# Attention heads and expert products on one TensorE: how far products may run ahead, and which engine splits the last weights

## The chip, the cores and the metric

The kernel runs on one core of one Trainium2 chip. The metric is the device time of one execution in microseconds; lower is better.

## The reference, cut to what matters

```python
# q, k, v: (4, 8, 576, 64) fp32, f: (4, 8, 576); w1: (4, 512, 1024), w2: (4, 1024, 512)
scores = q @ k.T / 8 + cum[:, None] - cum[None, :]      # cum = cumsum(log f), causal
attn = softmax(scores) ; a = attn @ v                     # 32 (batch, head) pairs
x = a with heads side by side: (2304, 512)
p = domain_probs / domain_probs.sum(-1)
out = sum over e of p[:, e] * (relu(x @ w1[e]) @ w2[e])   # 4 dense experts, 2304 tokens
```

## The kernel before

All matrix products are fp32 quality: each operand is split into a high part (a rounded copy, made on ScalarE) and a low part (the difference, made on VectorE or GpSimd), and three products high*high, high*low, low*high are summed in PSUM. TensorE therefore sees three matmuls for one, and the other engines make the parts.

Attention is cut into 64 heads, each a (batch, head) pair for one half of the queries: 32 early heads (half 0: the first 256 queries and keys) and 32 late heads (half 1: 320 queries against 576 keys). Two heads share one job, with one load of q and k (`load`, L235, into `raw`, one buffer) and one of v (L237). For a head, ScalarE copies the high part (L278), GpSimd casts q and makes the lower parts (L279, L287, L293), TensorE makes scores (L331), VectorE takes the minimum with the mask (L345), ScalarE the exponentials (L360), TensorE transposes (L423), ScalarE and VectorE split the result (L433, L440), TensorE multiplies with v (`av`, L473), and at the end of a job `fin` scales and stores the two heads.

Tokens lie in nine chunks of 256. Chunks 0 to 2 are multiplied directly while attention still runs: 48 steps (class `Step`), each a weight pair of one expert for one chunk, in eight quarter-steps (four `l1` at L639, four `l2` at L669), with a gate between on ScalarE and VectorE (L650, L651). Weights come in blocks of 1024 columns (`w_load`, L596, three buffers `wr`) and are split by `w_split`: the high part on ScalarE (L607), two lower halves of 128x512 on GpSimd or, for the blocks in W_DVE, on VectorE (L611). Six buffers hold split blocks (`wh`, `wl`); there are NS = 56 blocks. Chunks 3 to 5 and 6 to 8 form two sets. For a set `x_block` makes seven operands (four of them sums, L751 on GpSimd; high part L752, low part L753), and 16 weight pairs (class `Big`) follow, each with seven products of L815 and the second layer at L876. `big_split` makes a pair's weights: four sums on GpSimd (L769), high parts on ScalarE (L789), seven lower parts on GpSimd (L792), from the same three `wr` buffers and into the same six split buffers.

Order. The first eight heads (batch 0, half 0) run in `startup`, which is written out by hand slot by slot and keeps its order; its slots W_SLOT call `w_split` for blocks 0 to 3. After it the program order is made by `pace`: every piece of a head has a cost (an early head's `av` 1100, a late one's 600), and after each quarter-step as many pieces are emitted as the line through `marks` allows; all heads and the operands of set 0 are to be out AHEAD steps before the last. A scheduler then puts each engine's instructions in order by program order and by when it estimates them ready; each engine works its list in that order. `behind` ties each product to the heads: a quarter-step may be issued only after the last head instruction on TensorE that had been emitted LAG quarter-steps earlier. All DMAs are issued by SyncE in order.

Of the kernel before, what the change touches and what calls it, by code (L numbers as in the profile page):

```python
# [26 lines left out]
)  # L27
DIRECT = (0, 1, 2)
LEAD = 3
LAG = 5  # L30
W_DVE = tuple(range(4, 16, 2))
SETS = ((3, 4, 5), (6, 7, 8))
AHEAD = 4
W_SLOT = (5, 6, 7, 8)
NEAR = 2
JOBS = ((0, 0), (1, 0), (2, 0), (3, 0), (0, 1), (1, 1), (2, 1), (3, 1))

# [33 lines left out]
def fused(ctx: ExitStack, tc: tile.TileContext, qk, v, f, probs, w, out):  # L71
    nc = tc.nc
# [475 lines left out]
    heads = [(j, hh) for j in jobs for hh in range(2)]  # L548
    FIRST = 2 * NPR

    def head_steps(n):

        st = []
        if n + 1 < len(heads):
            j, hh = heads[n + 1]
            if hh == 0:
                st.append((0, j.prep_v))
            st.append((0, lambda j=j, hh=hh: j.prep(hh)))
        if n + 2 < len(heads):
            j, hh = heads[n + 2]  # L560
            st.append((0, lambda j=j, hh=hh: j.far(hh)))
        ahead = n + 2 < len(heads) and heads[n + 2][1] == 0
        if ahead:
            st.append((0, heads[n + 2][0].load))
        qs, ts, us = [], [], []
        if n < len(heads):
            j, hh = heads[n]
            for t in j.its:
                qs.append((TOK0[t] + 328, lambda j=j, hh=hh, t=t: j.qk_tile(hh, t)))
            if hh == 1:  # L570
                qs.append((0, j.recip))
        if n > FIRST:
            j, hh = heads[n - 1]
            for gi in range(len(j.blocks())):
                ts.append((500, lambda j=j, hh=hh, gi=gi: j.tr(hh, gi)))
            us.append(((1100, 600)[j.half], lambda j=j, hh=hh: j.av(hh)))
            if hh == 1:
                us.append((0, j.fin))
        if n + 1 < len(heads):
            j, hh = heads[n + 1]  # L580
            us.append((0, lambda j=j, hh=hh: j.begin(hh)))
        for k in range(max(len(qs), len(ts))):
            st += ts[k : k + 1] + qs[k : k + 1]
        return st + us
# [4 lines left out]
    NS = 4 * len(UNITS)  # L589
# [3 lines left out]
    def w_load(n):  # L593
        if n < NW and n not in wraw:
            wraw[n] = wr_p.tile([128, 1024], F32, tag="wr", name=f"wr{n}")
            nc.sync.dma_start(out=wraw[n], in_=w[ROWS[n]])  # L596

    def w_split(n):
        if n >= NS:
            if n % 2 == 0:  # L600
                big_split((n - NS) // 2)
            return
        w_load(n)
        wh[n] = w_p.tile([128, 1024], F32R, tag="wh", name=f"wh{n}")
        wl[n] = w_p.tile([128, 1024], F32R, tag="wl", name=f"wl{n}")
        r = wraw.pop(n)
        nc.scalar.activation(out=wh[n], in_=r, func=AF.Copy)  # L607
        for a in (0, 512):
            z = a + 512
            eng = nc.vector if n in W_DVE else nc.gpsimd  # L610
            i = eng.tensor_tensor(  # L611
                out=wl[n][:, a:z], in0=r[:, a:z], in1=wh[n][:, a:z].bitcast(F32), op=ALU.subtract
            )
            if eng is nc.gpsimd:
                latest["POOL"] = i
        w_load(n + 1)
        w_load(n + 2)
        w_load(n + 3)
# [118 lines left out]
    def x_block(n, k, a=None, z=None, op=None):  # L737

        hw = len(SETS[n]) * CH // 2
        hi = rh[n, k] = late.x.tile([128, 2, hw], F32R, tag=f"rh{k}", name=f"rh{n}_{len(rh)}")  # L740
        lo = rl[n, k] = late.x.tile([128, 2, hw], F32R, tag=f"rl{k}", name=f"rl{n}_{len(rl)}")
        x_of = lambda b: (
            xset[n][:, 2 * b[0] : 2 * b[0] + 2, hw * b[1] : hw * b[1] + hw]
            if type(b) is tuple
            else xs_[n, b]
        )
        if op is None:
            x = x_of(k)
        else:
            x = xs_[n, k] = late.x.tile([128, 2, hw], F32, tag="t", name=f"rx{n}_{k}", bufs=2)  # L750
            nc.gpsimd.tensor_tensor(out=x, in0=x_of(a), in1=x_of(z), op=op)  # L751
        nc.scalar.activation(out=hi, in_=x, func=AF.Copy)  # L752
        nc.vector.tensor_tensor(out=lo, in0=x, in1=hi.bitcast(F32), op=ALU.subtract)  # L753

# [3 lines left out]
    def big_split(p):  # L758
        if p >= 16 * len(SETS):
            return  # L760
        n = NS + 2 * p
        w_load(n)
        w_load(n + 1)
        r = [wraw.pop(n), wraw.pop(n + 1)]
        part = lambda b: r[b[0]][:, 256 * b[1] : 256 * b[1] + 256]
        t = late.x.tile([128, 4, 256], F32, tag="wt", name=f"wt{p}", bufs=1)
        w_of = lambda b: part(b) if type(b) is tuple else t[:, b - 1, :]
        for k, a, z, op in SUMS:
            nc.gpsimd.tensor_tensor(out=t[:, k - 1, :], in0=w_of(a), in1=w_of(z), op=op)  # L769
        tiles = []  # L770
        for k in range(3):
            tiles.append(
                [
                    w_p.tile([128, 1024], F32R, tag=x, name=f"b{x}{p}_{k}") for x in ("wh", "wl")
                ]
            )
        f = t.rearrange("p k n -> p (k n)")
        jobs_ = [
            (0, 0, f),
            (1, 0, part((1, 1))),  # L780
            (1, 256, part((0, 0))),
            (1, 512, part((0, 1))),
            (2, 0, r[0][:, 512:]),
            (2, 512, r[1][:, 512:]),
        ]
        for k, c, x in jobs_:
            w_ = x.shape[1]
            hi, lo = (y[:, c : c + w_] for y in tiles[k])
            nc.scalar.activation(out=hi, in_=x, func=AF.Copy)  # L789
            for a in range(0, w_, 512):  # L790
                z = min(a + 512, w_)
                nc.gpsimd.tensor_tensor(  # L792
                    out=lo[:, a:z], in0=x[:, a:z], in1=hi[:, a:z].bitcast(F32), op=ALU.subtract
                )
        bw[p] = tiles
        for k in range(2, 5):
            w_load(n + k)
# [103 lines left out]
    for x in X_ORDER:  # L901
        asteps.append((600, lambda x=x: x_block(0, *x)))
# [21 lines left out]
    goals = sorted((max(n - LEAD, 1), cost[need[c]]) for c, n in first.items() if n > 0)  # L924
    goals.append((len(steps) - AHEAD, cost[-1]))
    while goals:
# [17 lines left out]
    def startup():  # L944

        J = lambda h: heads[h] if 0 <= h < FIRST else (None, None)
        decays()
        for h in range(2):
            j, hh = J(h)
            if h == 0:  # L950
                j.prep_v()
            j.prep(hh)
        for h in range(2):
            J(h)[0].begin(h)
        heads[0][0].qk_pe(0, (0, 1))
        heads[0][0].qk_min(0, 0)
        heads[0][0].qk_min(0, 1)
        for s in range(FIRST + 2):
            (j, hh), (m, mm), (n, nn), (i, ii) = J(s), J(s + 1), J(s + 2), J(s - 2)
            if n:  # L960
                n.begin(nn)
                n.prep_hi(nn)
                n.prep_lo(nn)
            if m:
                m.qk_pe(mm, m.its)
                for t in m.its:
                    m.qk_min(mm, t)
            if j:
                for t in j.its:
                    j.qk_exp(hh, t)  # L970
            if i:
                i.av_pe(ii)
                i.av_top(ii)
                i.av_add(ii)
            if j:
                j.tr_pe(hh, 0)
                j.tr_hi(hh, 0)
                j.tr_lo(hh, 0)
                if hh == 1:
                    j.recip()  # L980
                if hh == 0 and s > 0:
                    j.prep_v()
            if s >= 5 and s % 2 == 1:
                heads[s - 4][0].fin()
            if s == FIRST + 1:
                heads[FIRST - 1][0].fin()
            if s in W_SLOT:
                w_split(W_SLOT.index(s))

    pt0 = [pt_p.tile([128, 1216], F32R, tag=x, name=f"{x}_first") for x in ("pth", "ptl")]  # L990
    with tc.manual_schedule():
        startup()

    with ExitStack() as after:
        for e in ("ACT", "DVE", "POOL"):
            i = latest[e]
            after.enter_context(tc.issue_after(i.ins))
        normalize()
        j = heads[FIRST][0]
        j.prep_v()  # L1000
        j.prep(0)
        j.begin(0)
        for n in range(len(W_SLOT), 6):
            w_split(n)
# [5 lines left out]
    def behind(act, q):  # L1010
        marks_pe.append(latest["PE"])
        with tc.issue_after(marks_pe[-min(len(marks_pe), LAG)].ins):
            act(q)
# [85 lines left out]
```

## Time and profile before

| | us |
|---|---|
| median of three runs (1040.11 to 1044.52) | 1042.0 |
| the profiled execution | 1039.19 |
| its span, first to last instruction | 1036.9 |
| TensorE busy | 982.1 (95%) |
| TensorE weight load busy | 882.5 (85%) |
| VectorE busy | 724.6 (70%) |
| GpSimd busy | 650.6 (63%) |
| ScalarE busy | 529.7 (51%) |
| mean granted TensorE clock | 0.988 |

The span is what the trace covers; the profiled execution is 2.3 us longer than its span, and the median of the runs is 2.8 us above the profiled execution. Busy time of TensorE counts a matmul until its modelled end, so a stretch that is fully busy may still hold small gaps: work is better counted in matmuls times their spacing.

### The profile page before, as it was taken

What the parts mean: (1) busy time and instruction counts of PE and PEld (TensorE: products, weight loads), DVE (VectorE), ACT (ScalarE), POOL (GpSimd) and SP (SyncE); (2) the same over time, 40 slices, a digit from 0 to 9 for tenths busy, and PEclk for the clock granted to TensorE, in tenths of its full rate; (3) what the DMA queues carried; (4) which work ended last, traced back from release to release, by engine and by line L of the source; (5) the groups of instructions that cost most, each with busy time, mean ns of one, the idle gap of its engine ahead of it and who ended that gap; (6) DMA issues with size and microseconds to landing.
All of it is one profiled execution on the core that took longest, in us unless ns stands there. A gap on an engine that the chain in (4) does not pass through costs nothing.

```text
span 1036.9 us, 15930 instructions
## 1 busy us (share of the span) xinstructions
PE 982.1 (95%) x5584; PEld 882.5 (85%) x5584; DVE 724.6 (70%) x1474; ACT 529.7 (51%) x1127; POOL 650.6 (63%) x690
## 2 busy tenths in 40 slices
PE   5788999999999999999699999999999999999998
PEld 4676878899998989999589887898988988988987
DVE  5668766676767777766447758766797777677665
ACT  6666767676766667675224333433343333433330
POOL 5756778563635475563977767676686766666640
PEclk9988999999999999999989999999999999999999
DMA  5344554342432343331321222112123222122101
GB/s 199 104 156 129 165 156 143 106 143 85 144 104 91 103 157 99 103 118 42 122 81 58 66 82 82 63 61 82 51 72 113 71 82 79 44 82 71 52 21 61
DMA packets 33903, 99.53 MB, mean 96 GB/s; under 512 B 3652, under 2 KB 5760, under 8 KB 33824
## 3 DMA queue, kind: packets, MB, share of 16 engines
q1 hardware_dynamic: 33824, 98.53, 29.2%
q8 instruction: 44, 0.72, 0.3%
q14 instruction: 35, 0.29, 0.1%
HBM read 93.64 MB, written 4.87 MB: 95 GB/s over the span
## 4 chain that ended last, share of the span: by engine, by line
PE 71%; POOL 7%; DVE 7%; issue 5%; ACT 5%; DMA 4%; SPq 0%; POOLq 0%; ACTq 0%; DVEq 0%
PE y L876 23%; PE m L815 20%; PE l L669 8%; PE l L639 7%; PE s L331 4%; PE t L423 4%; PE o L473 4%; DMA raw<-in_qk 2%; POOL wl L611 2%; POOL bwl L792 2%; DMA wr<-in_w 1%; ACT wh L607 1%; POOL wt L769 1%; ACT p L360 1%; DVE v L266 1%
## 5 line engine op out<-in xcount | busy, mean ns | idle before, releaser
L792 POOL TENSOR_TENSOR bwl<-wr,bwh 128x256 fp32r<-128x256 f32 (+1 forms) x160 | 166.3, 1065 | 31.2 <-ACT bwh L789 31.2
L691 DVE SCALAR_TENSOR_TENSOR acc<-y,prob,acc 128x512 f32<-128x512 f32 x180 | 130.4, 744 | 61.2 <-PE y L876 61.0
L815 PE MATMUL m<-rh,bwh 128*128 128x384 f32 x448 | 152.8, 341 | 7.6 <-ACT bwh L789 7.6
L876 PE MATMUL y<-bwh,hh 128*128 128x512 f32 x384 | 152.1, 396 | 2.6 <-DVE acc L691 2.6
L815 PE MATMUL m<-rl,bwh 128*128 128x384 f32 x448 | 152.1, 340 | 0.0
L876 PE MATMUL y<-bwl,hh 128*128 128x512 f32 x384 | 151.9, 396 | 0.0
L815 PE MATMUL m<-rh,bwl 128*128 128x384 f32 x448 | 150.5, 339 | 1.0 <-POOL bwl L792 1.0
L876 PE MATMUL y<-bwh,hl 128*128 128x512 f32 x384 | 150.2, 395 | 0.0
L611 POOL TENSOR_TENSOR wl<-wr,wh 128x512 fp32r<-128x512 f32 x100 | 132.3, 1348 | 25.9 <-ACT wh L607 20.0
L833 DVE TENSOR_TENSOR u<-m,u 128x384 f32<-128x384 f32 x192 | 105.1, 553 | 48.6 <-PE m L815 24.5
L845 DVE SCALAR_TENSOR_TENSOR hl<-u,hh 128x384 fp32r<-128x384 f32 x128 | 111.5, 893 | 32.3 <-ACT hh L844 32.0
L360 ACT ACTIVATE p<-p,nm 128x576 f32<-128x576 f32 (+2 forms) x160 | 95.9, 600 | 55.8 <-DVE nm L345 55.1
L844 ACT ACTIVATE hh<-u 128x384 fp32r<-128x384 f32 x128 | 65.2, 522 | 105.5 <-DVE u L833 105.4
L639 PE MATMUL l<-xh,wh 128*128 128x256 f32 x384 | 113.8, 297 | 2.0 <-ACT xh L520 2.0
L639 PE MATMUL l<-xh,wl 128*128 128x256 f32 x384 | 109.8, 286 | 0.8 <-POOL wl L611 0.8
L639 PE MATMUL l<-xl,wh 128*128 128x256 f32 x384 | 109.3, 285 | 0.5 <-DVE xl L523 0.4
L279 POOL CAST q<-raw 64x320 fp32r<-64x320 f32 (+1 forms) x56 | 24.7, 444 | 129.9 <-PE s L331 93.7
L792 POOL TENSOR_TENSOR bwl<-wt,bwh 128x512 fp32r<-128x512 f32 x64 | 81.6, 1296 | 37.5 <-ACT bwh L789 37.5
L815 PEld LDWEIGHTS m<-rh,bwh 128*128 128x128 f32 x448 | 85.2, 190 | 13.9 <-ACT bwh L789 8.5
L423 PE MATMUL t<-ident,p 128*128 128x128 f32 x480 | 85.1, 286 | 6.1 <-ACT p L360 4.8
L345 DVE CUSTOM_DVE_ANT_0 p<-s,mask 128x288 f32<-128x288 f32 (+2 forms) x160 | 74.8, 477 | 20.1 <-PE s L331 18.7
L815 PEld LDWEIGHTS m<-rl,bwh 128*128 128x128 f32 x448 | 85.3, 190 | 4.1
(102 smaller groups left out, 2387.0 us busy)
## 6 DMA issues: line engine op xcount, KB each, us to landing
wr<-in_w SPq DMA_DIRECT2D x120, 512.0 KB
raw<-in_qk SPq DMA_DIRECT2D x16, 896.0 KB
raw<-in_qk SPq DMA_DIRECT2D x12, 512.0 KB
vr<-in_v SPq DMA_DIRECT2D x16, 320.0 KB
out<-acc SPq DMA_DIRECT2D x16, 256.0 KB
first<-in_qk SPq DMA_DIRECT2D x4, 512.0 KB
vr<-in_v SPq DMA_DIRECT2D x12, 128.0 KB
first<-in_v SPq DMA_DIRECT2D x1, 512.0 KB
```

What stands on the lines that cost most here:

```text
L345: nc.vector.tensor_tensor_reduce(out=pt[:, a:z], in0=ps, in1=mask[:, m0 + a : m0 + z], scale=-0.125, scalar=BIG if n == 0 else nm[:, col : ...
L360: nc.scalar.activation(out=pt[:, :w_], in_=pt[:, :w_], func=AF.Exp, scale=-1.0, bias=self.nmax[hh][:, c : c + 1], accum_out=self.ssum[:, h ...
L423: latest["PE"] = nc.tensor.transpose(ps[:, at : at + 128], self.p[hh, it][:, TOK0[jt] : TOK0[jt] + 128], ident)
L611: i = eng.tensor_tensor(out=wl[n][:, a:z], in0=r[:, a:z], in1=wh[n][:, a:z].bitcast(F32), op=ALU.subtract)
L639: nc.tensor.matmul(out=self.l1p[:, fi, :], lhsT=lhsT, rhs=rhs[:, k, :], start=(k == 0 and m == 0), stop=(k == 3 and m == 2),)
L669: nc.tensor.matmul(out=l2[tt], lhsT=lhsT, rhs=rhs, start=(self.ps == 0 and fi == 0 and m == 0), stop=(self.ps == 1 and fi == 1 and m == 2),)
L691: nc.vector.scalar_tensor_tensor(out=acc[c][:, tt, :], in0=ps, scalar=sc, in1=acc[c][:, tt, :], op0=ALU.mult, op1=ALU.add,)
L792: nc.gpsimd.tensor_tensor(out=lo[:, a:z], in0=x[:, a:z], in1=hi[:, a:z].bitcast(F32), op=ALU.subtract)
L815: nc.tensor.matmul(out=ps, lhsT=lhsT[:, o], rhs=rhs[:, k, :], start=(k == 0 and i == 0), stop=(k == 1 and i == 2),)
L833: nc.vector.tensor_tensor(out=out, in0=a, in1=z, op=op)
L845: nc.vector.scalar_tensor_tensor(out=lo, in0=x, scalar=0.0, in1=hi.bitcast(F32), op0=ALU.max, op1=ALU.subtract)
L876: nc.tensor.matmul(out=ps, lhsT=lhsT, rhs=rhs, start=(fi == 0 and m == 0), stop=(fi == 1 and m == 2),)
```

## The change

`LAG` goes from 5 to 17, so a product may stand up to 17 quarter-steps (two steps) ahead of heads. The cost of an early head's `av` in `pace` goes from 1100 to 3600, `AHEAD` from 4 to 6. The weight splits in startup stand in slots 4, 5, 7, 9 in place of 5, 6, 7, 8 and at other places of the slot. The lower halves of the last six weight blocks (50 to 55), the four sums of set 0 and the lower parts of the first two weight pairs go from GpSimd to VectorE. The first `prep_v` comes after the first two `prep`.

```diff
-LAG = 5
+LAG = 17
-AHEAD = 4
-W_SLOT = (5, 6, 7, 8)
+AHEAD = 6
+W_SLOT = (4, 5, 7, 9)
...
-            us.append(((1100, 600)[j.half], lambda j=j, hh=hh: j.av(hh)))
+            us.append(((3600, 600)[j.half], lambda j=j, hh=hh: j.av(hh)))
...
-            eng = nc.vector if n in W_DVE else nc.gpsimd
+            eng = nc.vector if n in W_DVE or n >= NS - 6 else nc.gpsimd
...
-            nc.gpsimd.tensor_tensor(out=x, in0=x_of(a), in1=x_of(z), op=op)
+            eng = nc.vector if n == 0 else nc.gpsimd
+            eng.tensor_tensor(out=x, in0=x_of(a), in1=x_of(z), op=op)
...
-                nc.gpsimd.tensor_tensor(
+                eng = nc.vector if p < 2 else nc.gpsimd
+                eng.tensor_tensor(
...
         for h in range(2):
             j, hh = J(h)
-            if h == 0:
-                j.prep_v()
             j.prep(hh)
+        heads[0][0].prep_v()
...
                 for t in j.its:
                     j.qk_exp(hh, t)
+            if s == W_SLOT[0]:
+                w_split(0)
             if i:
                 i.av_pe(ii)
...
                 if hh == 0 and s > 0:
                     j.prep_v()
+            if s in W_SLOT[1:3]:
+                w_split(W_SLOT.index(s))
             if s >= 5 and s % 2 == 1:
                 heads[s - 4][0].fin()
-            if s == FIRST + 1:
+            if s == W_SLOT[3]:
+                w_split(3)
                 heads[FIRST - 1][0].fin()
-            if s in W_SLOT:
-                w_split(W_SLOT.index(s))
```

## Rows read from the trace of the kernel before

**Rows 1.** Busy time by stretch: start:end, length, engines, TensorE clock, DMA share, GB/s.
```profile
0.00:50.00 50.00, 31.78 (x132) 27.02 (x133) 28.91 (x92) 33.79 (x87) 30.77 (x49) 1.00 0.45 148
50.00:200.00 150.00, 133.69 (x868) 118.06 (x867) 105.45 (x281) 103.81 (x262) 99.30 (x124) 0.95 0.47 151
200.00:450.00 250.00, 247.94 (x1712) 229.43 (x1711) 181.26 (x474) 175.83 (x367) 136.58 (x138) 1.00 0.35 114
...
485.00:535.00 50.00, 39.28 (x204) 34.40 (x203) 24.84 (x29) 19.53 (x32) 45.16 (x35) 0.92 0.29 95
535.00:1037.00 502.00, 494.42 (x2435) 441.13 (x2434) 361.12 (x542) 175.79 (x342) 327.84 (x337) 1.00 0.21 69
```

**Rows 2.** TensorE's instructions by line, 50 to 200 us; count, busy, mean ns.
```profile
L639 PE MATMUL l<-xh,wh 128*128 128x256 f32 x118 | 34.1, 289 | 0.0
...
L669 PE MATMUL l<-wh,gh 128*128 128x512 f32 x58 | 25.7, 443 | 0.0
...
L423 PE MATMUL t<-ident,p 128*128 128x128 f32 x96 | 19.3, 285 | 0.9 <-ACT p L360 0.8
```

**Rows 3.** The same, 200 to 450 us.
```profile
L639 PE MATMUL l<-xh,wh 128*128 128x256 f32 x200 | 59.1, 295 | 0.0
...
L423 PE MATMUL t<-ident,p 128*128 128x128 f32 x317 | 50.6, 275 | 1.8 <-DVE xf L536 0.9 <-ACT p L360 0.7
```

**Rows 4.** The chain that ended last, 36 to 130 us: start, length, what.
```profile
105.59 0.46 PE s L331 x4
106.05 0.57 PE o L473 x4
106.62 1.42 PE l L669 x6
108.04 0.71 PE l L639 x6
```

**Rows 5.** The same chain, around the first loads of early heads.
```profile
49.81 5.34 DMA raw<-in_qk
...
59.55 3.96 DMA raw<-in_qk
```

**Rows 6.** The same chain, 476 to 540 us: the passage from steps to pairs.
```profile
502.00 5.75 POOL wl L611 x4
507.75 3.59 POOL rx L751 x2
...
519.07 4.58 POOL bwl L792 x5
...
523.67 3.43 DMA wr<-in_w
```

**Rows 7.** Lines L611, L753, L751 whole run: ns min/median/max, first and last start.
```profile
L611 POOL TENSOR_TENSOR wl<-wr,wh x100: 1255/1292/2021, 31.6 to 506.5; 128x512 fp32r<-128x512 f32 x100
...
L611 DVE TENSOR_TENSOR wl<-wr,wh x12: 678/692/1569, 47.4 to 109.9; 128x512 fp32r<-128x512 f32 x12
...
L753 DVE TENSOR_TENSOR rl<-xf,rh x6: 1010/1528/2602, 485.4 to 767.2; 128x768 fp32r<-128x768 f32 x6
...
L751 POOL TENSOR_TENSOR rx<-xf x4: 1826/2005/2564, 485.5 to 769.9; 128x768 f32<-128x768 f32 x4
```

**Rows 8.** VectorE's instructions by line, whole run; count, busy, mean ns.
```profile
L651 DVE SCALAR_TENSOR_TENSOR gl<-l,gh 128x512 fp32r<-128x512 f32 x48 | 32.9, 685 | 20.4 <-ACT gh L650 20.2
L691 DVE SCALAR_TENSOR_TENSOR acc<-l,prob,acc 128x512 f32<-128x512 f32 x42 | 31.2, 745 | 6.1 <-PE l L669 6.0
```

**Rows 9.** The chain that ended last, 590 to 635 us.
```profile
591.91 5.61 POOL bwl L792 x5
...
607.32 5.59 POOL bwl L792 x5
```

**Rows 10.** ScalarE's instructions in order of time, end of startup.
```profile
40.15 1.04 ACT L607 ACTIVATE wh<-wr 128x1024 fp32r<-128x1024 f32 x1
...
44.30 0.42 ACT L520 ACTIVATE xh<-xs 128x256 fp32r<-128x256 f32 x1 [1.34 <-DVE xs L514]
```

## The prediction

> **What bounds the kernel now.** First the busy time by stretch [rows 1]. TensorE is the busiest engine everywhere, and from 535 us to the end it is the bound: 494.4 of 502 us at full clock. There the change only touches the first pairs. From 200 to 450 us it is busy 247.9 of 250. The reader is to see three stretches where it is not the bound: 0 to 50 us (31.8 of 50), 50 to 200 us (133.7 of 150 at a clock of 0.95) and 485 to 535 us (39.3 of 50 at 0.92).
>
> A busy TensorE still hides gaps, so for 50 to 200 us I count work. A step takes four l1 quarters of 0.71 us and four l2 quarters, two in 1.42 us [rows 4], so 5.68 us. In the stretch stand 3 x 118 first-layer matmuls and 3 x 58 second-layer ones [rows 2], 24 and 12 to a step: 14.6 steps, 83 us. An early head takes 0.46 us for scores, 0.57 us for its product with v [rows 4] and some four 128-column transposes of about 0.1 us (a quarter of those 0.46 us, an estimate), so 1.45 us. The 96 transposes [rows 2] are 26 early heads of 3 and about a late head and a half of 12: 38 + 6 us. Together 127 of 150 us: **23 us are lost**, some of them to matmuls at the lower rate (a mean clock of 0.95 [rows 1] is a tenth of the stretch at 1.2 instead of 2.4 GHz).
>
> Why they are lost there and not later: before, 24 early heads fall on 13 of the 48 steps. The chain shows what a job of two such heads hangs on: its load of raw takes 5.34 us, and the next one starts 9.7 us after the first [rows 5], since there is one raw buffer. With 13 x 5.68 + 24 x 1.45 = 109 us, TensorE would want a head every 4.5 us, 9 us a job, and the job cannot come faster than that chain of 9.7. Products may stand only five quarters (3.6 us) ahead of late heads, so TensorE waits with them.
>
> From 485 to 535 us GpSimd is the bound, 45.2 of 50 [rows 1]. The chain [rows 6] is its queue: lower halves of weights (5.75 us for four), sums (3.59 us for two), lower parts of the first pair (4.58 us for five), then a load of 3.43 us that waited for their buffer. TensorE lacks 10.7 us there, and a clock of 0.92 (a sixth of the stretch at the lower level) costs some 2 more: 13 us.
>
> **The change, part by part.** The sum is made against the profiled execution: span 1036.9, time 1039.2. The median of the runs is 2.8 us above that.
>
> *Startup.* The last split of block 3 (1.04 us on ScalarE [rows 10]) stands ahead of the last early head's copies and goes to slot 9, between the two last fins, where ScalarE waits 1.34 us for VectorE anyway [rows 10]. One split more in slot 4 meets a ScalarE that is busy 33.8 of 50 [rows 1]. `w_split` brings up to three loads on SP's queue with it. They move up with the buffer that they wait for, and the raw loads behind them are due after startup. The moved `prep_v` lets the first high part start earlier, but the rows of decays for the third head come from a chain of DMAs that it does not touch: nothing. I take -1 us (0 to -2).
>
> *Early heads, pace and LAG.* I followed `pace` through by its costs. The 24 early heads end in step 19 instead of 13 and all heads in step 41 instead of 43. So 18.5 steps go with them: 18.5 x 5.68 + 24 x 1.45 = 140 us, 5.8 us a head, 11.7 us a job, above the 9.7 us of the chain. Products up to 12 us ahead cover a late head. The cover itself: the steps brought forward want about 8 blocks more in that time. GpSimd, at 2 x 1.29 us a block [rows 7], goes from 99 to 120 of 150 us; the steps' gates (0.685 [rows 8]) and sums (0.745) take VectorE from 105 to 113; DMA share goes from 0.47 to some 0.56 [rows 1]. It holds, but not with much to spare. If it fails, products wait for weights and the 23 us stay. If all goes well 2 us are left. Between the two I take 6 left, as the 200 to 450 us row, with room of this kind, loses little: **-17 us** (-4 to -21).
>
> *Late heads.* 32 of them now fall on 22 steps instead of 30. From 200 to 450 us TensorE did 25 steps (3 x 200 matmuls, 24 to a step [rows 3]), 142 us, and 26.4 heads (317 transposes), so a late head takes (250 - 142) / 26.4 = 4.1 us with its stalls. The work is the same, its mix denser: 22 x 5.68 + 32 x 4.1 = 256 us. VectorE worked 181.3 us there [rows 1], of which the steps had 25 x 1.43 = 36 [rows 8], so 5.5 us a head. It now wants 32 x 5.5 + 22 x 1.43 = 207 of 256 us, 81% where it had 73. More waits in its queue are what comes late next: scores' minima, the split of the transposes. **+4 us** (0 to +30).
>
> *The passage.* Twelve lower halves (1.29 us each on GpSimd), four sums (2.0) [rows 7] and 14 lower parts leave GpSimd; for the two pairs it keeps the sums of weights. VectorE gets them. Lower halves have a row there: 0.69 us at the median, 1.57 at most [rows 7]. For a sum the nearest row is the low part of the same 128x768, 1.01 to 2.60, median 1.53 [rows 7]. For pairs I scale the first by columns: 2816 columns are 5.5 times 512, 3.8 to 8.6 us a pair. With AHEAD = 6, six steps are left after the last head, 34 us of TensorE. Beside them VectorE has gates and accumulations 6 x 1.43 = 8.6, low parts 7 x 1.53 = 10.7, sums 4 x 1.53 = 6.1, halves 12 x 0.69 = 8.3 and pair 0 3.8: 37.5 us. At the lowest prices it is 32, at the highest 65. I take the medians, since GpSimd has then little to do. So VectorE and TensorE are level there and some 4 us of the 13 remain: **-9 us** (-12 to +13). Queued behind these on VectorE are gates and accumulations, for which TensorE waits.
>
> One thing speaks against taking the low price. The rows show the same half at 0.68 and at 1.57 us and the same low part at 1.01 and 2.60 on VectorE [rows 7]. The Trainium skill, "SBUF — State Buffer", section "Who interferes with whom", says that a VectorE instruction with two SBUF inputs contends with a GpSimd instruction that reads SBUF, and that whichever issues first holds the shared ports for its whole instruction. By that rule the moved work is cheap just as far as GpSimd is idle beside it; where it is not, the passage comes out as the second rival below.
>
> *First pairs.* From 590 us on a chain of 15.4 us a pair (591.91 to 607.32 [rows 9]) is on the path: lower parts, load, sums. Pairs 0 and 1 made faster put it ahead of TensorE. TensorE is idle 7.6 of the 502 us after 535 us [rows 1], and I give 2 of them to this: **-2 us** (0 to -3).
>
> Sum: -1 - 17 + 4 - 9 - 2 = -25. Span 1012, execution 1014.2, median **1017 us**.
>
> **Rivals.**
> 1. Products do not run ahead. The change permits it, but six split buffers hold three steps' weights, and an order made from estimates may leave heads where they are late. For it: each gap in the early stretch is small, which an order fixed beforehand would give again. Against: the products' share of the stretch is what `pace` gave them. Then of the -17 only the -4 stay: 1030 us.
> 2. The moved work contends on VectorE. Half of it at the high price makes 51 us against 34 of TensorE, so 17 idle instead of 4: 1030 us too. For: the maxima in [rows 7]. Against: GpSimd loses most of its queue there.
> 3. VectorE becomes the bound under the late heads: slower. Its queue is in order and full of waits; if it cannot be busier than the 0.70 it had from 50 to 200 us [rows 1], 207 us of work take 296 instead of 256, 36 more than I took: 1053 us. It decides from a share of about 0.72 downward (207 / 0.72 = 288, which is 28 us more than I took and eats the gain of 25); at 0.73, which it had from 200 to 450 us, there is next to no change. Against: there TensorE, not VectorE, was the bound.
> 4. All covers hold: -2 - 21 + 0 - 12 - 3 = -38, 1004 us.
>
> **How the numbers follow.** My forecast 0.52, rival 1 0.16, rival 2 0.12, rival 3 0.08, rival 4 0.12. A measurement of this kernel can tell about 0.5%, 5.2 us. The forecast, rivals 1, 2 and 4 lie below 1036.8 except for a tail of each, 0.06 in all, that the wide bounds of the late heads' term bring within 0.5%. Rival 3 splits: 0.06 slower, 0.02 the same. So faster 0.86, same 0.08, slower 0.06. The range takes in rivals 1, 2 and most of 4, and leaves out half of rival 3's tail and the far end of 4: 1002 to 1037.
>
> **What would show it.** Right: product rows of 50 to 200 us counted at near 18 steps instead of 14.6, with the clock at 1.00; the last head ending near 460 us and steps after it; in the passage VectorE near full, GpSimd half idle, less than 6 us of TensorE lost; the second set's first product some 25 us earlier. Wrong: the count of steps there unchanged (rival 1); halves and sums on VectorE above 1.2 us with gates behind them (rival 2); VectorE at or below 0.73 under late heads, with TensorE waiting for its minima (rival 3).

## The result, and the profile after

The changed kernel takes 1015.9 us (median of four runs, 1015.12 to 1016.27) against 1041.2 us for the kernel before on the same chip: ratio 0.9751, 95% interval 0.9727 to 0.9775. The forecast was 1017, range 1002 to 1037. The profiled execution of the changed kernel took 1016.24 us, its span 1014.4, so 22.5 us of span have gone. One execution of all the versions below, of the one with LAG 16, took 3330.2 us and is left out of its median.

Busy time by stretch, changed kernel, columns as in [rows 1]:

```profile
0.00:50.00 50.00, 33.11 (x156) 27.85 (x157) 34.10 (x91) 34.19 (x87) 31.30 (x49) 1.00 0.45 150
50.00:200.00 150.00, 144.44 (x988) 132.58 (x987) 102.81 (x266) 100.24 (x244) 103.77 (x124) 0.99 0.48 156
200.00:450.00 250.00, 242.64 (x1653) 219.70 (x1653) 192.62 (x516) 187.00 (x398) 141.06 (x145) 1.00 0.36 116
...
485.00:535.00 50.00, 46.42 (x231) 41.69 (x230) 36.70 (x63) 18.22 (x35) 23.10 (x24) 0.93 0.31 103
```

Beside [rows 1] the reader is to see four things. From 50 to 200 us TensorE ran 988 matmuls instead of 868, at a clock of 0.99 instead of 0.95. From 200 to 450 us it ran fewer, 1653 instead of 1712, and was busy 242.6 instead of 247.9: something was given back there. In the passage TensorE is busy 46.4 of 50 instead of 39.3, GpSimd 23.1 instead of 45.2, and VectorE 36.7 instead of 24.8. The granted clock of the passage (485 to 535 us) is 0.93, against 0.92.

The clock of 1.00 in both first rows is not what the matmuls show. In the kernel before, those of 256 columns start 0.213 us apart until 48.3 us:

```profile
47.28 0.41 PE L639 MATMUL l<-xh,wh 128*128 128x256 f32 x1
47.49 0.41 PE L639 MATMUL l<-xl,wh 128*128 128x256 f32 x1
```

In the changed kernel they start 0.12 us apart from 39.6 us on, with waits between:

```profile
45.54 0.28 PE L639 MATMUL l<-xh,wh 128*128 128x256 f32 x1
45.66 0.28 PE L639 MATMUL l<-xl,wh 128*128 128x256 f32 x1
```

So TensorE starts at the lower of its two levels (1.2 of 2.4 GHz) here, and in the changed kernel it leaves it some 9 us sooner. With LAG back at 5 (first experiment) the spacing at 45 us is 0.213 us again. Part of what 0 to 50 us gains is this.

The products of the early stretch, same kernel, against [rows 2]:

```profile
L639 PE MATMUL l<-xh,wh 128*128 128x256 f32 x156 | 44.7, 287 | 0.0
...
L669 PE MATMUL l<-wh,gh 128*128 128x512 f32 x77 | 31.2, 406 | 0.0
```

3 x 156 over 24 and 3 x 77 over 12 are 19.4 steps, where 14.6 stood.

To compare versions, the table counts work as the prediction did, as matmuls of a stretch times their spacing in dense runs (0.1176, 0.175 and 0.2325 us for 256, 384 and 512 columns, 0.1 for a transpose, 5 ns and 0.45 ns a column for other shapes), and gives what is missing to the length of the stretch. It prices the small matmuls of early heads lower than the prediction's 1.45 us a head, so before shows 34 us missing in the early stretch, not 23; differences between versions depend on it little. Matmuls at the lower clock count as missing too. "Missing" below is this number. Line numbers move by up to five between versions.

| TensorE time without work, us | 0 to 50 | 50 to 200 | 200 to 450 | 450 to 650 | time, us |
|---|---|---|---|---|---|
| before | 36.9 | 33.6 | 6.3 | 18.7 | 1041.2 |
| changed | 33.1 | 12.4 | 18.2 | 9.8 | 1015.9 |
| changed, LAG 5 | 36.4 | 15.8 | 14.6 | 1.5 | 1010.7 |
| changed, LAG 16 | 33.8 | 13.8 | 13.7 | 6.6 | 1011.1 |
| changed, cost 1100 | 33.8 | 29.4 | 7.6 | 8.8 | 1022.9 |
| changed, AHEAD 4 | 33.1 | 11.8 | 12.7 | 14.4 | 1015.1 |
| changed, engines back | 32.9 | 12.6 | 18.3 | 17.2 | 1024.3 |
| changed, startup back | 35.5 | 7.6 | 17.6 | 9.6 | 1010.9 |
| changed, set 1's sums later | 33.4 | 12.8 | 17.4 | 5.2 | 1011.4 |
| before, LAG 17 | 35.6 | 21.9 | 5.6 | 16.1 | 1022.8 |
| before, spread and AHEAD 6 | 37.2 | 14.5 | 13.5 | 11.0 | 1020.3 |
| startup and engines only | 36.4 | 40.2 | 6.6 | 9.5 | 1035.5 |

From before to changed: -3.8, -21.2, +11.9, -8.9, which is -22.0 of the span's 22.5.

### The profile page after: what moved, and what is told of

It reads as the page before. It is cut to its first block, busy times and chain, and to the rows that moved or that the text cites. A ratio compares the mean times of both kernels' runs of the same rounds, so it can differ in the third digit from the quotient of the medians.

```text
span 1014.4 us, 15921 instructions
## 1 busy us (share of the span) xinstructions
PE 973.8 (96%) x5584; PEld 874.7 (86%) x5584; DVE 738.9 (73%) x1504; ACT 529.8 (52%) x1127; POOL 609.4 (60%) x660
## 4 chain that ended last, share of the span: by engine, by line
PE 71%; DVE 9%; ACT 5%; DMA 5%; issue 5%; POOL 3%; SPq 0%; ACTq 0%; POOLq 0%; DVEq 0%
PE y L878 25%; PE m L817 22%; PE l L669 7%; PE l L639 7%; DMA raw<-in_qk 5%; PE s L331 4%; PE t L423 3%; PE o L473 3%; DVE v L266 2%; ACT hi L278 1%; ACT p L360 1%; DVE p L345 1%; POOL kl L287 1%; ACT wh L607 1%; POOL hi L293 1%
## 5 line engine op out<-in xcount | busy, mean ns | idle before, releaser
L794 POOL TENSOR_TENSOR bwl<-wr,bwh 128x256 fp32r<-128x256 f32 (+1 forms) x150 | 155.6, 1065 | 36.6 <-ACT bwh L790 36.6
L835 DVE TENSOR_TENSOR u<-m,u 128x384 f32<-128x384 f32 x192 | 105.1, 554 | 40.2 <-PE m L817 24.8
L611 POOL TENSOR_TENSOR wl<-wr,wh 128x512 fp32r<-128x512 f32 x88 | 113.1, 1309 | 27.7 <-ACT wh L607 14.7
L639 PE MATMUL l<-xh,wh 128*128 128x256 f32 x384 | 111.7, 292 | 1.0 <-ACT xh L520 0.9
L345 DVE CUSTOM_DVE_ANT_0 p<-s,mask 128x288 f32<-128x288 f32 (+2 forms) x160 | 75.2, 477 | 32.9 <-PE s L331 31.8
L794 POOL TENSOR_TENSOR bwl<-wt,bwh 128x512 fp32r<-128x512 f32 x60 | 76.4, 1296 | 35.1 <-ACT bwh L790 34.0
L770 POOL TENSOR_TENSOR wt<-wr 128x256 f32<-128x256 f32 x32 | 23.9, 748 | 109.7 <-DMA wr<-in_w 83.0
```

The lines of the kernel that those rows point to most:

```text
L345: nc.vector.tensor_tensor_reduce(out=pt[:, a:z], in0=ps, in1=mask[:, m0 + a : m0 + z], scale=-0.125, scalar=BIG if n == 0 else nm[:, col : ...
L611: i = eng.tensor_tensor(out=wl[n][:, a:z], in0=r[:, a:z], in1=wh[n][:, a:z].bitcast(F32), op=ALU.subtract)
L639: nc.tensor.matmul(out=self.l1p[:, fi, :], lhsT=lhsT, rhs=rhs[:, k, :], start=(k == 0 and m == 0), stop=(k == 3 and m == 2),)
L794: eng.tensor_tensor(out=lo[:, a:z], in0=x[:, a:z], in1=hi[:, a:z].bitcast(F32), op=ALU.subtract)
L835: nc.vector.tensor_tensor(out=out, in0=a, in1=z, op=op)
```

## The experiments

Each ratio is to the kernel before, run on the same chip; the time of a version and that of the changed kernel may come from two chips, on which the kernel before took 1040.3 to 1042.1 us.

**LAG alone, out of the change.**

```diff
-LAG = 17
+LAG = 5
```

> The changed kernel with LAG back at 5; all else changed. If products standing far ahead of heads is what fills TensorE from 50 to 200 us, the time comes back by 6 to 14 us (1022 to 1030), with fewer product matmuls in that stretch than the changed kernel's 156 + 156 + 156 of the first layer. Rival: the spread of early heads alone does it, LAG only permits what nobody uses: within 3 us of 1016.

Measured: 1010.7 us (ratio 0.9713, 0.9688 to 0.9739), 5.2 us faster than the changed kernel, so both expectations missed: neither a loss nor no difference. The early stretch loses only 3.4 us by it (15.8 against 12.4): the spread of heads, not LAG, had filled it. What comes back is in the passage. The last head's output ends at 477.6 us in the changed kernel (first line) and at 466.3 with LAG 5 (second):

```profile
477.05 0.55 DVE L536 TENSOR_TENSOR xf<-xs,b 128x64 f32<-128x64 f32 x2
465.75 0.55 DVE L536 TENSOR_TENSOR xf<-xs,b 128x64 f32<-128x64 f32 x2
```

TensorE's instructions from there, first the changed kernel (477.6 to 500 us):

```profile
L669 PE MATMUL l<-wh,gh 128*128 128x512 f32 x16 | 6.3, 396 | 0.2 <-DVE acc L691 0.2
...
L639 PE MATMUL l<-xh,wh 128*128 128x256 f32 x18 | 5.0, 279 | 0.0
...
L817 PE MATMUL m<-rh,bwh 128*128 128x384 f32 x1 | 0.7, 689 | 3.2 <-ACT bwh L790 3.2
```

and the one with LAG 5 (466.3 to 500 us; by 560 us L669's x22 is x24):

```profile
L639 PE MATMUL l<-xh,wh 128*128 128x256 f32 x40 | 11.2, 279 | 0.0
...
L669 PE MATMUL l<-wh,gh 128*128 128x512 f32 x22 | 8.7, 396 | 0.7 <-DVE acc L691 0.7
...
L817 PE MATMUL m<-rl,bwh 128*128 128x384 f32 x8 | 2.7, 337 | 0.0
```

With LAG 17, 3 x 18 and 3 x 16 step matmuls were left behind the last head, 17.5 us by their spacing; with LAG 5, 3 x 40 and 3 x 24, 31 us. Such products are the cover of the passage: they keep TensorE at work while the first pairs' operands are made. Those that ran ahead of heads are no longer there when the passage needs them, and the last head itself ends 11 us later. The 3.2 us wait for the first pair's weights stands in the first and not in the second.

The wait costs more than itself. After it the first 384-column matmuls of the changed kernel start 0.32 us apart, from 506 us on 0.175:

```profile
500.50 0.52 PE L817 MATMUL m<-rl,bwh 128*128 128x384 f32 x1
500.82 0.52 PE L817 MATMUL m<-rh,bwl 128*128 128x384 f32 x1
...
506.11 0.33 PE L817 MATMUL m<-rl,bwh 128*128 128x384 f32 x1
506.28 0.34 PE L817 MATMUL m<-rh,bwl 128*128 128x384 f32 x1
```

TensorE stood idle and came back at the lower clock: 0.93 granted from 485 to 535 us, 3.5 us of the 50, where the version with LAG 5 has 1.00. A change of LAG from 17 to 16 moves the time as much as this one (below), so it is these rows, not the 5 us, that show what LAG takes from the passage.

**The spread of early heads, out of the change.**

```diff
-            us.append(((3600, 600)[j.half], ...
+            us.append(((1100, 600)[j.half], ...
```

> The changed kernel with the early head's cost back at 1100, so early heads fall on some 13 steps again and late heads on 29; LAG stays at 17. If early heads are late because of their own chain of loads, products can be at most 12 us ahead and TensorE waits from 50 to 200 us again, while late heads lose less: 1020 to 1032. Rival: LAG alone covers late heads; then early heads on 13 steps cost nothing, the late heads' 11 us of loss goes away, and the time is 1005 to 1014.

Measured: 1022.9 us (0.9834, 0.981 to 0.9857), as the theory had it. The early stretch misses 29.4 us again, with LAG at 17, and the late stretch falls from 18.2 to 7.6. Products there, 50 to 200 us:

```profile
L639 PE MATMUL l<-xh,wh 128*128 128x256 f32 x120 | 36.1, 301 | 0.0
```

120 to an operand pair, next to the 118 of [rows 2]. The closer comparison is the version with startup and engines only (below), which has LAG 5 and AHEAD 4 in place of 17 and 6:

```profile
L639 PE MATMUL l<-xh,wh 128*128 128x256 f32 x108 | 33.6, 311 | 0.0
```

So LAG does add products when the program order asks for heads first, 12 of each kind, and takes 11 us off what is missing there (40.2 to 29.4). The spread adds far more: the changed kernel, with both, has 156.

**The moves to VectorE, out of the change.**

```diff
-            eng = nc.vector if n in W_DVE or n >= NS - 6 else nc.gpsimd
+            eng = nc.vector if n in W_DVE else nc.gpsimd
-            eng = nc.vector if n == 0 else nc.gpsimd
+            eng = nc.gpsimd
-                eng = nc.vector if p < 2 else nc.gpsimd
+                eng = nc.gpsimd
```

> The changed kernel with the last six blocks' halves, set 0's sums and the first two pairs' lower parts back on GpSimd. If GpSimd's queue bounds the passage, 9 to 16 us come back (1025 to 1032), with GpSimd near full between the last head and the first pair. Rival: AHEAD = 6 and the earlier end of heads alone relieve the passage: 1016 to 1020.

Measured: 1024.3 us (0.9846, 0.9819 to 0.9873), 8.4 us back, just under the band, and nearly all of it in the passage (9.8 to 17.2). Busy time from 465 to 500 us, first the changed kernel:

```profile
465.00:500.00 35.00, 30.93 (x187) 27.10 (x187) 27.43 (x43) 16.95 (x24) 7.18 (x6) 0.98 0.32 106
```

then this one:

```profile
465.00:500.00 35.00, 31.47 (x188) 26.95 (x186) 21.96 (x25) 15.03 (x20) 30.11 (x19) 1.00 0.27 91
```

GpSimd goes from 7.2 to 30.1 of 35 us. It bounds the passage even with the heads ending early.

**Startup, out of the change.**

```diff
-W_SLOT = (4, 5, 7, 9)
+W_SLOT = (5, 6, 7, 8)
...
+            if h == 0:
+                j.prep_v()
             j.prep(hh)
-        heads[0][0].prep_v()
```

(and the four calls of `w_split` back at the end of their slots.)

> The changed kernel with startup as before (slots 5 to 8, the first prep_v ahead of the first prep). By the windows of the two traces startup gave 3.7 us of TensorE's idle time from 25 to 50 us, more than the 1 us forecast: 1018 to 1021. Rival: those 3.7 us are products that run ahead by LAG after startup, and startup itself gives nothing: 1015 to 1017.

Measured: 1010.9 us (0.9718, 0.9693 to 0.9744), 5 us faster than the changed kernel; both expectations missed. The profiled execution, which the table counts, took 1013.3 us, so the table shows some 3 of the 5. Startup does lose 2.4 us by it (35.5 against 33.1), but the early stretch then misses 7.6 instead of 12.4. TensorE's waits there go from 5.5 us to 2.1 in all (those for ScalarE's exponentials and splits from 4.1 to 0.2), and the granted clock from 0.99 to 1.00; what in the order does that was not found. With LAG 5 (below) startup makes no difference that can be told.

**LAG alone, put into the kernel before.**

```diff
-LAG = 5
+LAG = 17
```

> The kernel before with LAG 17 and nothing else changed. The undoing of LAG in the changed kernel cost nothing (it was 5 us faster), so the theory now is that LAG lets products fill the early stretch and takes the same products away as cover for the passage after the last head, where the chain of weights sets the time: 1036 to 1044 against 1040. The theory on record, that it frees time by itself: 1022 to 1032.

Measured: 1022.8 us (0.9819, 0.9795 to 0.9842), inside the band of the theory on record and not of the one formed from the first experiment. With the tight order of before, LAG is worth 18 us, 11.7 of them in the early stretch, where the 118 of [rows 2] become 129.

**The spread alone, put into the kernel before.**

```diff
-AHEAD = 4
+AHEAD = 6
-            us.append(((1100, 600)[j.half], ...
+            us.append(((3600, 600)[j.half], ...
```

> The kernel before with the early head's cost 3600 and AHEAD 6 alone; LAG 5, startup and engines as before. If the spread alone is what fills the early stretch and LAG is a substitute for it, 1018 to 1027, with some 16 us of TensorE's work missing from 50 to 200 us where before misses 34, and a full GpSimd in the passage. Rival: it needs LAG 17 or the moved work to be worth anything: 1030 to 1041.

Measured: 1020.3 us (0.9799, 0.9777 to 0.9821), as expected. Its early products, 50 to 200 us:

```profile
L639 PE MATMUL l<-xh,wh 128*128 128x256 f32 x154 | 44.0, 285 | 0.0
```

154, nearly the changed kernel's 156, with LAG at 5. So LAG (-18) and the spread with AHEAD (-22) are substitutes in part: each mends the waiting for early heads (33.6 us missing become 21.9 and 14.5), and both together, with the rest of the change, leave 12.4.

**Only startup and engines.**

```diff
-LAG = 17
+LAG = 5
-AHEAD = 6
+AHEAD = 4
-            us.append(((3600, 600)[j.half], ...
+            us.append(((1100, 600)[j.half], ...
```

> The changed kernel with LAG, the early head's cost and AHEAD as before, so only startup and the move of work from GpSimd to VectorE are left of the change. If the moves are worth what their undoing cost (8.4 us) and the spread of early heads the rest, 1029 to 1034, with some 33 us of TensorE's work still missing from 50 to 200 us. Rival: the passage is worth all of it once products stand behind heads as before: 1014 to 1024.

Measured: 1035.5 us (0.9958, 0.9936 to 0.998), nearer to the theory, some 1.5 us above its band. The passage improves by 9.2 us (18.7 to 9.5), and 6.6 of them are lost in the early stretch, which misses 40.2, at a granted clock of 0.91 where before has 0.95 (6 us of the 150). LAG, spread and AHEAD together are then worth 19.6 us.

**Set 1's sums later.**

```diff
+                if n == 1:
+                    behind_split.enter_context(tc.issue_after(latest["SPLIT", 4].ins))
                 eng.tensor_tensor(out=x, in0=x_of(a), in1=x_of(z), op=op)
```

> The changed kernel with the four sums of set 1 on GpSimd ordered behind the lower parts of pair 4. In the changed kernel two of them (1.83 us each) stand in GpSimd's queue between the four sums of the first pair's weights, and TensorE waits 3.2 us for that pair right after. If that queue is the wait: 1012 to 1014. Rival: the loads of the first pair's weights or the buffers they wait for set it, and the sums only fill a pause: 1015 to 1017.

Measured: 1011.4 us (0.9715, 0.9687 to 0.9744), 4.5 us faster than the changed kernel, just under the first band. GpSimd's instructions in order of time, changed kernel:

```profile
490.44 0.74 POOL L770 TENSOR_TENSOR wt<-wr 128x256 f32<-128x256 f32 x1 [26.64 <-DVE acc L691]
491.13 1.53 POOL L770 TENSOR_TENSOR wt<-wr,wr 128x256 f32<-128x256 f32 x1
492.63 1.83 POOL L752 TENSOR_TENSOR rx<-xf 128x768 f32<-128x768 f32 x1
494.42 0.73 POOL L770 TENSOR_TENSOR wt<-wt,wr 128x256 f32<-128x256 f32 x1
495.11 1.83 POOL L752 TENSOR_TENSOR rx<-xf,rx 128x768 f32<-128x768 f32 x1
496.90 0.72 POOL L770 TENSOR_TENSOR wt<-wr,wt 128x256 f32<-128x256 f32 x1
```

and here:

```profile
491.19 1.46 POOL L773 TENSOR_TENSOR wt<-wr 128x256 f32<-128x256 f32 x1 [27.40 <-DVE acc L691]
492.62 0.73 POOL L773 TENSOR_TENSOR wt<-wr,wr 128x256 f32<-128x256 f32 x1
493.31 0.73 POOL L773 TENSOR_TENSOR wt<-wt,wr 128x256 f32<-128x256 f32 x1
494.12 0.74 POOL L773 TENSOR_TENSOR wt<-wr,wt 128x256 f32<-128x256 f32 x1
```

GpSimd had been idle for 26 us, yet the two sums of set 1, not wanted for some 250 us, were put between the four sums that the first pair hangs on. Without them those end 2.8 us sooner. TensorE's waits for the first pairs from 455 to 530 us, changed kernel and here:

```profile
PE m L817 <- ACT bwh L790: 3.6, 2, 3.2
PE m L820 <- ACT bwh L793: 2.0, 2, 1.6
```

That is 1.6 us less. The clock gives the rest: from 485 to 535 us it is 1.00 here, where the changed kernel has 0.93:

```profile
485.00:535.00 50.00, 48.02 (x254) 43.06 (x253) 40.17 (x67) 20.79 (x41) 22.74 (x25) 1.00 0.31 104
```

**A change of no substance.**

```diff
-LAG = 17
+LAG = 16
```

> The changed kernel with LAG 16 in place of 17: a change of no substance, to see how much the time moves with the order that the scheduler happens to make. If order alone moves little: 1014 to 1018. If the differences of 5 us between variants are such chance, it may lie anywhere from 1009 to 1023.

Measured: 1011.1 us (0.9716, 0.9679 to 0.9753), 4.8 us from the changed kernel and outside the narrow band. The order that the scheduler makes moves the time by about that much by itself. So single differences of 4 to 5 us here are not put down to their edit unless a row shows the place.

**AHEAD alone, out of the change.**

```diff
-AHEAD = 6
+AHEAD = 4
```

> The changed kernel with AHEAD at 4: heads end two steps later. Late heads get more room, so less of the 16 us that TensorE loses from 200 to 450 us, but two steps fewer cover the passage: 1014 to 1024. Rival: the late heads' loss comes from their number per step and two steps more free it, and the passage does not need the cover: 1006 to 1013.

Measured: 1015.1 us (0.9742, 0.972 to 0.9765). The cover half of the theory shows: the passage misses 14.4 instead of 9.8. The step matmuls left behind the last head are 8 us of TensorE here, 17.5 in the changed kernel, 22 with LAG 16 and 31 with LAG 5, and the passage misses 14.4, 9.8, 6.6 and 1.5. The other half is not shown: the late stretch misses 12.7 instead of 18.2, but LAG 16, which gives late heads no more room, has 13.7.

**Three edits together.** LAG 5, startup as before and set 1's sums later, by the diffs above.

> The changed kernel with LAG 5, startup as before and set 1's sums behind pair 4, three edits that were each 4 to 5 us faster alone. If they act on different stretches they add up in part: 1001 to 1007. Rival: LAG 5 and the later sums mend the same wait ahead of the first pair, and startup's 5 us needs products that run ahead: 1007 to 1013.

Measured: 1011.5 us (0.9711, 0.9691 to 0.973): the rival. With LAG 5 the passage has enough cover (1.7 us missing from 450 to 650 us; 1.5 with LAG 5 alone), so the later sums mend nothing more.

**A smaller spread.** LAG 5, set 1's sums later, and

```diff
-            us.append(((3600, 600)[j.half], ...
+            us.append(((2600, 600)[j.half], ...
```

> The changed kernel with LAG 5, set 1's sums behind pair 4 and the early head's cost at 2600, so early heads end some two steps sooner and late heads get more room. If late heads' loss falls by more than the early stretch gives back: 1003 to 1009. Rival: the early stretch gives back more: 1010 to 1018.

Measured: 1013.8 us (0.9734, 0.9716 to 0.9752): the rival. From 50 to 200 us 20.2 us are missing, against 15.8 with LAG 5 and the full spread, at a granted clock of 0.97 against 0.99; from 200 to 450 us 13.8 against 14.6.

No combination went below the 1010.7 us of LAG 5 alone. Five versions (LAG 5, LAG 16, startup back, later sums, the three together) lie between 1010.7 and 1011.5 us, 4 to 5 below the changed kernel, and these runs do not tell them apart.

## Why the prediction was right, and where its steps were not

The time came out 1 us from the forecast, and that is in part luck. Startup and early heads gave 7 us more than forecast, late heads cost 8 more and the passage gave 2 less, so the span fell by 22.5 us and not 25; and the 2.8 us that the sum added from the profiled execution to the median were not there for the changed kernel (1016.24 and 1015.9).

*Early heads, pace and LAG* (-17): measured -21.2 by the table. The reading of the stretch held: 19.4 steps where "near 18" was forecast, at a clock of 0.99. But the step "Products up to 12 us ahead cover a late head" had the wrong cause for this kernel. With the spread in place LAG 17 added 3.4 us there; the spread alone fills the stretch, and LAG is the other, weaker way to the same end. **Rival 1**, that products do not run ahead, fell: LAG alone brings 129 in place of 118 and the spread alone 154.

What made early heads late before is argued and not shown: no run gave `raw` a second buffer, so the chain of loads of 9.7 us a job stands untested. The largest waits that TensorE had from 50 to 200 us were for the split of the transposes, before and then changed:

```profile
PE o L473 <- DVE ptl L440: 6.2, 6, 2.1
PE o L473 <- ACT pth L433: 3.4, 2, 2.7
...
PE t L423 <- ACT p L360: 2.1, 2, 1.8
PE o L473 <- ACT pth L433: 2.0, 1, 2.0
```

*Late heads* (+4): mis-sized, +11.9. The range reached to +30. VectorE's share is 192.6 of 250, 0.77, between 0.73 before and the forecast 0.81, so **rival 3** fell. The engines' queues do make TensorE wait more; its waits from 200 to 450 us:

```profile
PE t L423 <- ACT p L360: 2.2, 4, 0.9
PE t L423 <- DVE xf L536: 1.7, 3, 1.2
PE s L331 <- DVE pth L448: 1.0, 1, 1.0
```

Before, the longest total there was 0.9 us. These are exponentials, outputs and splits of heads. The prediction named VectorE's queue; the largest wait is for ScalarE, which the sum did not price. All waits of the stretch are 6.8 us in the changed kernel and 1.9 before, so they show 4.9 of the 11.9; the rest lies in gaps shorter than the modelled end of a matmul and was not located. That the spread causes the loss is shown by the table: the four versions with cost 1100 miss 5.6 to 7.6 us there, the eight with 3600 12.7 to 18.3. What moves it within these eight was not found.

*The passage* (-9) *and first pairs* (-2): -8.9 together, against -11. Undoing the moves cost 8.4 us of time. The prices were right at the low end. VectorE's rows in the changed kernel:

```profile
L754 DVE TENSOR_TENSOR rl<-xf,rh 128x768 fp32r<-128x768 f32 x6 | 7.3, 1227 | 1.7 <-ACT rh L753 1.6
...
L794 DVE TENSOR_TENSOR bwl<-wt,bwh 128x512 fp32r<-128x512 f32 x4 | 2.6, 689 | 2.2 <-ACT bwh L790 2.2
...
L794 DVE TENSOR_TENSOR bwl<-wr,bwh 128x256 fp32r<-128x256 f32 x6 | 2.2, 418 | 0.0
L752 DVE TENSOR_TENSOR rx<-xf 128x768 f32<-128x768 f32 x2 | 1.9, 954 | 0.0
```

0.69 us for 512 columns, 0.42 for 256, 0.95 for a sum and 1.23 on the mean for a low part, where 0.69 and, for the last two, 1.53 had been taken. **Rival 2** fell. The step that failed is "six steps are left after the last head, 34 us of TensorE": 17.5 us were left, since LAG had let TensorE spend the rest, and the last head, forecast near 460 us, ended at 477.6. VectorE, forecast near full there, was busy 36.7 of 50 us. The clock did not come back either: 0.93 granted, 0.92 before. And the prediction counted set 0's sums out of GpSimd's queue without asking which of set 1's would move up into the gap. On pairs, the wait from 600 to 650 us went (3.4 to nothing), and some 3 us more are missing from 550 to 600.

*Startup* (-1): -3.8 from 0 to 50 us, but most of it comes with LAG: with LAG 5 the stretch misses 36.4. Startup's own part there is 0.5 us with LAG 5 (36.9 before, 36.4 with startup and engines only) and 2.4 with LAG 17, near the forecast. The runs put no gain in time on it: undone it was 5 us faster with LAG 17, and 0.7 us slower in the version with LAG 5 (which also had set 1's sums later). Its worth in time stays open, within the 5 us that order alone makes.

So the -25 of the forecast and the -22.5 measured agree in size, but the parts are others. On top of startup and engines (1035.5), LAG with AHEAD is worth 12.6 us of time (1022.9), the spread with AHEAD 24.8 (1010.7) and all three 19.6; the moves 8.4; startup not told apart.

## What to carry to other kernels

Filler work that may run ahead is a stock: what it fills early it cannot cover later, so before loosening such a bound look for the next place that lives on the same stock. Two edits that mend the same wait do not add up; put each alone into the old kernel, as well as taking each out of the new one. When an engine's queue is relieved, ask what the scheduler will hoist into the gap, and count a stretch's work in matmuls times spacing, as busy time hides half of the loss or more (16 us idle from 50 to 200 us before, 34 missing). And a wait of 3 us can cost as much again when TensorE comes back at the lower clock.

## What was not expected of the hardware

GpSimd's sum of 128x768 took 1.83 us in the changed kernel, where VectorE had only accumulations beside it, but twice that and more in the version with LAG 5, where VectorE was making low parts and halves without slowing down. GpSimd's rows there:

```profile
476.23 3.67 POOL L752 TENSOR_TENSOR rx<-xf 128x768 f32<-128x768 f32 x1 [19.45 <-DVE rl L754]
479.97 4.22 POOL L752 TENSOR_TENSOR rx<-xf,rx 128x768 f32<-128x768 f32 x1
490.08 0.73 POOL L770 TENSOR_TENSOR wt<-wr 128x256 f32<-128x256 f32 x1 [5.89 <-DMA wr<-in_w]
```

and VectorE's beside them:

```profile
476.01 1.28 DVE L611 TENSOR_TENSOR wl<-wr,wh 128x512 fp32r<-128x512 f32 x2
477.22 0.94 DVE L754 TENSOR_TENSOR rl<-rx,rh 128x768 fp32r<-128x768 f32 x1
...
480.01 2.48 DVE L611 TENSOR_TENSOR wl<-wr,wh 128x512 fp32r<-128x512 f32 x4
```

These low parts and halves cover 1.9 us of the first sum and 2.5 us of the second. 1.83 us plus these is 3.7 and 4.3, where 3.67 and 4.22 were measured: the sums took longer by about as long as VectorE did this work. The prediction had expected the moved work to suffer; here GpSimd did.

The Trainium skill, "SBUF — State Buffer", section "Who interferes with whom", says that whichever of the two issues first holds the shared ports and the other waits. The trace agrees that one of them waits in full, here GpSimd; the rule of who issued first it does not settle, as the second sum starts by its record 0.04 us ahead of VectorE's halves.
